# Feeding the first passes of a fused gated-MLP and spectral-filter kernel: two columns ahead of the rest, all their weights at once, the other columns transposed by DMA, and a deviation by square root and reciprocal

## The chip, the cores and the metric

One Trainium2 chip, one core. The time is the device time of one execution in microseconds (us), as the median of a kernel's runs. The profile gives one execution in full: its span is about 1.7 us shorter than the time. With each kernel under test the kernel before is run on the same chip, so each comparison has its own runs of before.

## The reference

```python
def reference(A_x, A_w_r, A_w_i, B_x, B_w_gate, B_w_up, B_w_down):   # helpers written inline
    x = A_x                                     # 1 x 2048 x 512, bf16
    xn = (x - mean(x)) / sqrt(var(x) + 1e-5)    # over the last axis
    X = rfft2(xn) * (w_r + 1j * w_i)            # spectral filter
    A = irfft2(X)
    g = xn @ B_w_gate                           # 512 x 1792
    u = xn @ B_w_up
    B = (gelu_tanh(g) * u) @ B_w_down           # 1792 x 512
    return x + A + B
```

The 2048 rows lie on 128 partitions in 16 "columns" of 128 rows. Both branches read the normalized rows: the gated MLP needs them transposed (`xnT`), the spectral branch reads them as they are, in four "folds" of four columns, and multiplies the folds (`xf`) with a table `RF_t` into `bp`.

## The kernel before

All five engines are planned by a small scheduler in the kernel: each operation has an estimated duration and a priority, the planner simulates the engines and the fetches, and the operations are emitted in the order that comes out. A changed estimate anywhere can therefore change the order of an engine much later. The parts that the change touches:

```python
    load_x(0, 1)
    d_ident = load_ct("ident", "ident", "ACT")
    load_x(1, 1)
    load_w(0, 2, ("SP", "ACT"))          # two chunks of gate and up weights a fetch
    add("ACT", 1.3, lambda: nc.scalar.activation(out=eps[:, 1:2], in_=eps[:, 0:1], func=AF.Gelu_apprx_tanh),
        (o_eps,), -900)                  # loads gelu's table early
    load_x(2, 2)
    load_w(2, 4)
    load_w(4, 6)
    load_x(4, 4)
    load_w(6, 10)
    load_x(8, 4)
    load_w(10, 14)
    # ... (cut)
    NWARM, NGAP, GAP = 10, 1, 4          # dummy matmuls: 10 of 512 at the start, 4 of 128 at column 0
    # ... (cut)
    def layernorm(c0, n, due, after=(), halves=1):
        # ... (cut: bn_stats and bn_aggr of each column, VectorE)
        e = dve(0.07, lambda: V.tensor_scalar(out=ve[:, k], in0=mv[:, k, 1], scalar1=EPS, ...), ag, due - 5)
        r = add("POOL", 0.55, lambda: nc.gpsimd.tensor_tensor(
            out=rstd[:, k], in0=ve[:, k], in1=half[:, k], op=ALU.pow), (e, o_mem[1]), due - 5, lag=0.1)
        # ... (cut: (x - mean) * rstd into xn, VectorE)
    # ... (cut: pe_transpose: four transposes into ONE tile, copied out by ScalarE and VectorE in halves)
    for c in range(4):
        if c == 2:
            layernorm(2, 2, -22, XT[0])
        pe_transpose(c, -28 + 3 * c)
        if c < NGAP:
            dummies(GAP, -29.9 + 3 * c, XN[c], P)
    for c0, n, due in ((4, 2, 14), (6, 2, 16), (8, 4, 24), (12, 4, 32)):
        layernorm(c0, n, due)
        for c in range(c0, c0 + n):
            dma_transpose(c, due)
        if c0 == 6:
            d_rf = load(P * NC * P * 2, lambda: nc.sync.dma_start(out=RF_t[:], ...), XN[7])
            load_x(12, 4, deps=XN[7])
    # ... (cut)
    FIRST = [(0, 1, 0, 4), (1, 1, 0, 4), (0, 2, 4, 2), (2, 2, 0, 2), (2, 2, 2, 2), (2, 2, 4, 2)]
    for c, n, f, nf in FIRST + [(0, 4, f, 1) for f in range(6, NFC)]:
        glu(c, n, f, nf)                 # (first column, columns, first chunk of 128, chunks)
```

## Time and profile before

| kernel before | value |
|---|---|
| median of its first 3 runs | 179.28 us (179.19 to 179.54) |
| span of the profiled run | 177.6 us |
| TensorE busy | 98% |
| first 256-wide matmul, from which TensorE is dense | 11.53 us |
| last matmul starts | 174.70 us, 163.17 us later |
| from there to the end | 2.9 us |

The page, the start and the pace of TensorE are shown and read in the prediction below. A timeline line reads: start, duration, engine, source line, operation, output<-input; in brackets how long the engine was idle before and what ended it.

### The profile page before, as it was taken

What the parts mean: (1) busy time and instruction counts of PE and PEld (TensorE: products, weight loads), DVE (VectorE), ACT (ScalarE), POOL (GpSimd) and SP (SyncE); (2) the same over time, 40 slices, a digit from 0 to 9 for tenths busy, and PEclk for the clock granted to TensorE, in tenths of its full rate; (3) what the DMA queues carried; (4) which work ended last, traced back from release to release, by engine and by line L of the source; (5) the groups of instructions that cost most, each with busy time, mean ns of one, the idle gap of its engine ahead of it and who ended that gap; (6) DMA issues with size and microseconds to landing.
All of it is one profiled execution on the core that took longest, in us unless ns stands there. A gap on an engine that the chain in (4) does not pass through costs nothing.

```text
span 177.6 us, 3041 instructions
## 1 busy us (share of the span) xinstructions
PE 173.4 (98%) x1100; PEld 92.9 (52%) x1100; DVE 118.1 (66%) x266; ACT 87.4 (49%) x158; POOL 18.6 (10%) x33
## 2 busy tenths in 40 slices
PE   6999999999999999999999999999999999999993
PEld 2598545545554544554555455554445444544463
DVE  1869999999537995889999885336442541632522
ACT  3162437456789737999998855453111211211100
POOL 3212138743200000000000000000000000000000
PEclk9999999999999999999999999999999999999999
DMA  5999487999297001302211121100222221322212
GB/s 144 311 355 359 86 270 84 223 296 193 52 347 255 2 0 29 93 2 59 61 48 37 37 59 37 27 0 0 84 68 66 83 89 59 92 80 69 74 45 59
DMA packets 23182, 19.24 MB, mean 108 GB/s; under 512 B 8512, under 2 KB 21824, under 8 KB 23168
## 3 DMA queue, kind: packets, MB, share of 16 engines
q1 hardware_dynamic: 22176, 17.57, 35.0%
q0 software_dynamic: 320, 1.19, 3.1%
q10 hardware_dynamic: 672, 0.30, 0.6%
q8 instruction: 8, 0.13, 0.3%
q14 instruction: 6, 0.05, 0.1%
HBM read 13.28 MB, written 2.10 MB: 87 GB/s over the span
## 4 chain that ended last, share of the span: by engine, by line
PE 91%; ACT 3%; DVE 3%; issue 1%; POOL 0%; DVEq 0%; POOLq 0%
PE u_ps L502 25%; PE g_ps L502 25%; PE warm L380 3%; ACT E L652 2%; PE yp L818 2%; PE bp L581 2%; PE gp L767 2%; PE yp__2078 L872 2%; PE yp__1994 L872 2%; PE yp__1967 L872 2%; PE yp__1936 L872 2%; PE yp__1909 L872 2%; PE yp__1820 L872 2%; PE yp__1793 L872 2%; PE yp__1762 L872 2%; PE yp__1735 L872 2%
## 5 line engine op out<-in xcount | busy, mean ns | idle before, releaser
L502 PE MATMUL g_ps<-xnT,Wg_sb 128*128 128x512 bf16 (+2 forms) x264 | 58.1, 347 | 0.0
L502 PE MATMUL u_ps<-xnT,Wu_sb 128*128 128x512 bf16 (+2 forms) x264 | 57.9, 347 | 0.0
L527 DVE TENSOR_TENSOR hT<-u_ps,ge 128x512 bf16<-128x512 f32 x56 | 38.4, 685 | 17.5 <-PE u_ps L502 14.4
L519 ACT ACTIVATE ge<-g_ps 128x512 bf16<-128x512 f32 x56 | 33.5, 598 | 30.5 <-PE g_ps L502 26.5
L502 PEld LDWEIGHTS <-Wu_sb 128*128 128x128 bf16 x264 | 24.3, 98 | 22.3 <-DMA Wu_sb<-in_B_w_up_dram 0.2
L502 PEld LDWEIGHTS <-Wg_sb 128*128 128x128 bf16 x264 | 24.3, 98 | 20.7 <-issue 0.2
L872 PEld LDWEIGHTS <-hT 128*128 128x128 bf16 x252 | 23.0, 98 | 21.9
L824 ACT CAST yf<-yp 128x512 bf16<-128x512 f32 x16 | 9.3, 586 | 37.6 <-PE yp L818 37.6
L652 ACT CAST E<-ep 64x512 bf16<-64x512 f32 x32 | 18.5, 579 | 1.1 <-PE ep L646 0.7
L396 DVE BATCH_NORM_STATS2 st<-x_t 128x6 f32<-128x512 bf16 x16 | 10.5, 676 | 4.8 <-DMA x_t<-in_A_x_dram 4.8
L629 ACT CAST ds<-dp 128x512 bf16<-128x512 f32 x16 | 8.8, 589 | 1.1 <-PE dp L624 1.0
L773 ACT CAST Gs<-gp 128x512 bf16<-128x512 f32 x16 | 8.6, 593 | 1.0 <-PE gp L767 1.0
L406 POOL TENSOR_TENSOR rstd<-ve,half 128x2 f32<-128x2 f32 (+2 forms) x7 | 6.6, 949 | 21.9 <-DVE ve L404 21.9
L585 ACT CAST Bs<-bp 128x512 bf16<-128x512 f32 x16 | 8.3, 603 | 0.5 <-PE bp L581 0.5
L818 PEld LDWEIGHTS <-Gs 128*128 128x128 bf16 x64 | 4.8, 98 | 3.5
L380 PE MATMUL warm<-warm 128*128 128x512 bf16 (+1 forms) x14 | 5.1, 539 | 1.3 <-POOL half L373 1.3
L412 DVE TENSOR_SCALAR xn<-x_t,mv,rstd 128x512 bf16<-128x512 bf16 (+1 forms) x17 | 6.1, 399 | 0.3 <-POOL rstd L406 0.3
L818 PE MATMUL yp<-CT,Gs 128*128 128x128 bf16 x64 | 6.0, 219 | 0.0
L683 DVE TENSOR_TENSOR m<-X,TW 128x1024 bf16<-128x1024 bf16 x8 | 5.5, 692 | 0.2
L624 PEld LDWEIGHTS <-Bs 128*128 128x128 bf16 x64 | 4.4, 98 | 2.4
L689 DVE TENSOR_TENSOR m<-X,TW 128x1024 bf16<-128x1024 bf16 x8 | 5.5, 684 | 0.0
L646 PE MATMUL ep<-ds,CT 128*128 128x512 bf16 x16 | 5.4, 379 | 0.0
(103 smaller groups left out, 169.0 us busy)
## 6 DMA issues: line engine op xcount, KB each, us to landing
y<-in_A_x_dram SPq DMA_DIRECT2D x16, 128.0 KB, 2.1
F<-F SPq DMA_DIRECT2D x32, 64.0 KB, 2.0
out_dram<-y SPq DMA_DIRECT2D x15, 128.0 KB, 1.7
Wd_sb<-in_B_w_down_dram SPq DMA_DIRECT2D x2, 896.0 KB, 8.3
x_t<-in_A_x_dram SPq DMA_DIRECT2D x3, 512.0 KB, 6.8
Wg_sb<-in_B_w_gate_dram SPq DMA_DIRECT2D x2, 512.0 KB, 6.8
Wu_sb<-in_B_w_up_dram SPq DMA_DIRECT2D x2, 512.0 KB, 9.1
Wg_sb<-in_B_w_gate_dram SPq DMA_DIRECT2D x3, 256.0 KB, 5.1
```

The costliest lines, as they stand in the source:

```text
L380: nc.tensor.matmul(tiles["warm"][:, 0:w], lhsT=warm[:, 0:P], rhs=warm[:, 0:w], start=True, stop=True)
L396: V.bn_stats(out=st[:], in_=x_t[:, c])
L502: nc.tensor.matmul(tiles[f"{nm}.{key}"][:, f * w:f * w + w], lhsT=W[:, e, (f0 + f) * P:(f0 + f + 1) * P], rhs=rhs(e), start=(f + e == 0), ...
L519: nc.scalar.activation(out=e[:, 0:nf * w], in_=tiles[f"g_ps.{key}"][:, 0:nf * w], func=AF.Gelu_apprx_tanh)
L527: V.tensor_tensor(out=out, in0=tiles[f"u_ps.{key}"][:, 0:nf * w].rearrange("p (f w) -> p f w", w=w) if nf > 1 else tiles[f"u_ps.{key}"][:, ...
L585: nc.scalar.copy(out=o, in_=tiles[f"bp.{cg}.{q}"][:].rearrange("p c (r g a) -> p (c r) g a", r=2, a=4))
L629: nc.scalar.copy(out=ds[:].rearrange("p (s k t) -> p s k t", s=2, t=2), in_=tiles[f"dp.{G}"][:].rearrange("p s t k -> p s k t"))
L652: nc.scalar.copy(out=tiles[f"E.{g}"][64 * h:64 * h + 64, r], in_=tiles[f"ep.{g}.{h}"][64 * r:64 * r + 64])
L773: nc.scalar.copy(out=o, in_=tiles[f"gp.{g}.{h}"][:].rearrange("p q (n a) -> p (q n) a", a=4))
L818: nc.tensor.matmul(yp[:, q], lhsT=tiles["G"][:, q, c], rhs=IQ[q], start=(q == 0), stop=(q == 3), skip_group_check=True)
L824: nc.scalar.copy(out=tiles[f"yf.{c // 2}"][:, c % 2], in_=tiles[f"yp.{c}"][:])
L872: nc.tensor.matmul(y[:, s], lhsT=tiles[sb, f][:, cl * P:(cl + 1) * P], rhs=Wd_sb[:, f, s], start=(f == 0), stop=False)
```

## The change

The intent: get TensorE dense sooner. Columns 0 and 1 come first with all 14 weight chunks (two columns wide after the first four), then columns 2 and 3 with all of theirs, two columns wide (the later blocks of four columns stay four wide); weights come in fetches of four chunks, gate ahead of up; column 0's deviation no longer goes through GpSimd's power; each half of a column has its own transpose tile; columns 2 and 3 are transposed by DMA instead of TensorE; x of columns 4 to 15 and `RF_t` are fetched after those transposes. Not shown in the cuts: in a pass of several chunks the matmuls of the first half of the contraction come first, the gathers of the filter's tables are planned behind the transposes of columns 12 to 15, and the weights of the last product (`Wd_sb`) come in one fetch.

```diff
-    def op(self, eng, dur, fn, deps=(), prio=0.0, new=(), use=(), lag=0.0, nbytes=0):
+    def op(self, eng, dur, fn, deps=(), prio=0.0, new=(), use=(), lag=0.0, nbytes=0, land=0.0):
 ... (cut: a fetch may be given the time at which the planner is to take it as landed)
-    load_x(2, 2)
-    load_w(2, 4)
-    load_w(4, 6)
-    load_x(4, 4)
-    load_w(6, 10)
-    load_x(8, 4)
-    load_w(10, 14)
+    d_g = [load_first(e, eng) for e, eng in ((0, "ACT"), (2, "SP"))]
+    add("ACT", 1.5, lambda: nc.scalar.activation(out=eps[:, 1:2], in_=eps[:, 0:1], func=AF.Sqrt), (o_eps,), -900)
+    d_u = load(NE * P * P * 4, lambda: nc.sync.dma_start(out=Wu_sb[:, :, 0:4 * P], ...), land=7.0)
+    load_w(4, 8, (8.4, 10.9), lambda: load_x(2, 2, 9.6))
+    load_w(8, 12, (12.2, 13.6))
+    load_w(12, 14, (14.3, 15.0))
 ... (cut)
-    NWARM, NGAP, GAP = 10, 1, 4
+    NWARM, NGAP, GAP = 8, 1, 2
 ... (cut)
+    def layernorm_sqrt(c, due, after=()):
+        s = dve(0.6, lambda: stats(c), [XD[c]] + list(after), due - 3.0)
+        a = dve(0.15, lambda: V.bn_aggr(out=mv[:, c], in_=tiles["st", c][:]), (s,), due - 3.2)
+        r = SD[c] = act(0.2, lambda: nc.scalar.activation(
+            out=rstd[:, c:c + 1], in_=mv[:, c, 1:2], func=AF.Sqrt, bias=eps[:, 0:1], scale=1.0), (a, o_eps), due - 60)
+        r = dve(0.07, lambda: V.reciprocal(out=rstd[:, c:c + 1], in_=rstd[:, c:c + 1]), (r,), due - 3.0)
 ... (cut: normalize in two halves; a transpose tile for each half)
+    layernorm_sqrt(0, -28)
+    layernorm_sqrt(1, -25, XN[0])
+    pe_transpose(0, -28)
+    dummies(GAP, -29.9, XN[0], P)
+    act(1.5, lambda: nc.scalar.activation(out=eps[:, 1:2], in_=eps[:, 0:1], func=AF.Gelu_apprx_tanh), [SD[1]] + XT[0], -70)
+    pe_transpose(1, -25, 1)
+    for c0, n, due in ((2, 2, -40), (4, 2, 14), (6, 2, 16), (8, 4, 24), (12, 4, 32)):
+        layernorm(c0, n, due, XN[max(c0 - 4, 1)])
         for c in range(c0, c0 + n):
             dma_transpose(c, due)
-        if c0 == 6:
+        if c0 == 2:
+            load_x(4, 4, 0.0, deps=XN[3], prio=-80.0)
+            load_x(8, 4, 0.0, deps=XN[3], prio=-80.0)
             d_rf = load(P * NC * P * 2, lambda: nc.sync.dma_start(
-                out=RF_t[:], ...), XN[7])
-            load_x(12, 4, deps=XN[7])
+                out=RF_t[:], ...), XN[3], prio=-80.0)
+            load_x(12, 4, 0.0, deps=XN[3], prio=-80.0)
 ... (cut)
-    FIRST = [(0, 1, 0, 4), (1, 1, 0, 4), (0, 2, 4, 2), (2, 2, 0, 2), (2, 2, 2, 2), (2, 2, 4, 2)]
-    for c, n, f, nf in FIRST + [(0, 4, f, 1) for f in range(6, NFC)]:
-        glu(c, n, f, nf)
+    for c in range(2):
+        glu(c, 1, 0, 4)
+    for f in range(4, NFC, 2):
+        glu(0, 2, f, 2)
+    for f in range(0, NFC, 2):
+        glu(2, 2, f, 2)
```

## The prediction

> **What bounds the kernel now.** I read the page first (busy shares, the strip of 40 slices, the chain by engine), then the groups by shape, then the timeline of TensorE alone over the first 60 us and the last ten, then the timeline of all engines over the first 9 us, last the DMA windows of 1 us.
>
> The page says that one engine is the kernel:
>
> ```profile
> PE 173.4 (98%) x1100; PEld 92.9 (52%) x1100; DVE 118.1 (66%) x266; ACT 87.4 (49%) x158; POOL 18.6 (10%) x33
> PE   6999999999999999999999999999999999999993
> PE 91%; ACT 3%; DVE 3%; issue 1%; POOL 0%; DVEq 0%; POOLq 0%
> ```
>
> TensorE has work from the first slice to the last, so only its own work, its start and the tail can matter. Its timeline shows where it becomes dense:
>
> ```profile
> 5.78 0.65 PE L428 MATMUL tp<-CT,xn 128*128 128x128 bf16 x4
> 6.23 0.63 PE L380 MATMUL warm<-warm 128*128 128x128 bf16 x4
> 6.89 0.82 PE L502 MATMUL g_ps<-xnT,Wg_sb 128*128 128x128 bf16 x8
> ...
> 10.19 0.61 PE L502 MATMUL g_ps<-xnT,Wg_sb 128*128 128x128 bf16 x8
> 10.64 0.61 PE L502 MATMUL u_ps<-xnT,Wu_sb 128*128 128x128 bf16 x8
> 11.09 0.61 PE L428 MATMUL tp<-CT,xn 128*128 128x128 bf16 x8
> 11.53 1.04 PE L502 MATMUL g_ps<-xnT,Wg_sb 128*128 128x256 bf16 x8
> 12.41 1.04 PE L502 MATMUL u_ps<-xnT,Wu_sb 128*128 128x256 bf16 x8
> ...
> 18.52 1.03 PE L502 MATMUL g_ps<-xnT,Wg_sb 128*128 128x512 bf16 x4
> 19.38 1.03 PE L502 MATMUL u_ps<-xnT,Wu_sb 128*128 128x512 bf16 x4
> ```
>
> The starts give the pace of one matmul (the durations overlap): 512 wide (19.38 - 18.52)/4 = 0.216 us, 256 wide (12.41 - 11.53)/8 = 0.109, 128 wide (10.64 - 10.19)/8 = 0.056. After 11.53 the program holds 641 matmuls of 512, 79 of 256 and 286 of 128: 138.3 + 8.6 + 15.9 = 162.8 us. The last one starts at 174.70, which is 163.2 us after 11.53. So there is no gap over 0.4 us in all behind 11.53; the tail from 174.70 to the end at 177.6 is 2.9 us (last add, last store). What can be won lies ahead of 11.53. There the first column's way to TensorE counts:
>
> ```profile
> 3.51 0.69 DVE L396 BATCH_NORM_STATS2 st<-x_t 128x6 f32<-128x512 bf16 x1 [3.51 <-DMA x_t<-in_A_x_dram]
> 4.23 0.18 DVE L403 BATCH_NORM_AGGREGATE mv<-st 128x2 f32<-128x6 f32 x1
> 4.45 0.15 DVE L404 TENSOR_SCALAR ve<-mv 128x1 f32<-128x1 f32 x1
> 4.52 0.69 DVE L396 BATCH_NORM_STATS2 st<-x_t 128x6 f32<-128x512 bf16 x1
> 4.76 0.58 POOL L406 TENSOR_TENSOR rstd<-ve,half 128x1 f32<-128x1 f32 x1 [2.70 <-DVE ve L404]
> 5.24 0.18 DVE L403 BATCH_NORM_AGGREGATE mv<-st 128x2 f32<-128x6 f32 x1
> 5.38 0.60 DVE L412 TENSOR_SCALAR xn<-x_t,mv,rstd 128x256 bf16<-128x256 bf16 x2
> ...
> 6.47 0.37 ACT L431 COPY xnT<-tp 128x256 bf16<-128x256 bf16 x1 [3.29 <-PE tp L428]
> 6.88 0.29 DVE L431 COPY xnT<-tp 128x256 bf16<-128x256 bf16 x1 [0.83 <-ACT xnT L431]
> ```
>
> From the aggregate (ends 4.41) to the normalization (5.38) are 0.97 us, for an add and a power on GpSimd. The two copies out of one transpose tile run one after the other: the first starts only when all four transposes are done (6.43), the second waits for the first. Column 1's statistics (4.52) hide inside the wait for GpSimd.
>
> **What the Trainium skill says.** "TensorE: Matmul & The Clock Gate", Part 1, says that the array runs at half clock until an activity window of about 3.4 us was busy, and that the window runs free. The trace agrees: the first warm-up matmuls start 0.43 us apart, twice 0.216, and the 128-wide ones go from 0.11 to 0.056 apart near 7.3 us, in the first eight of g_ps. "ScalarE: Activation LUTs", What ACT_TABLE_LOAD costs, gives 1283 ns for a load plus a drain of about 1380 ns, and about 280 ns for a small ACTIVATE whose bias is a pointer. The trace has one load, 1.28 us from 1.69, and its ACTIVATE at 2.98, so no drain is seen behind an empty engine; that ACTIVATE, with an immediate bias, takes 0.20 us. "DMA: Bandwidth & Descriptors", Anatomy of one DMA, puts about 2.0 us fixed on each transfer beside the bytes, on the GpSimd path; here, from SyncE, 512 KB alone land in 3.7 us (RF_t), of which 1.5 us are bytes at 0.36 MB/us: near 2.2 us.
>
> **The change part by part.**
>
> 1. Work of TensorE. After the narrow passes, columns 0 to 3 had four passes two columns wide and then eight chunks four wide; now all the rest is two wide. 64 matmuls of 512 (13.81 us) become 128 of 256 (13.96): +0.15 us. Eight transposes go to DMA: -8 x 0.056 = -0.45 us. Warm-up shrinks from 10+4 to 8+2, off the path.
>
> 2. Deviation of column 0. Aggregate ends 4.41; the square root on ScalarE starts near 4.48 and takes about 0.28 (the skill's figure for a pointer bias; 0.20 in the trace for an immediate); hop 0.06 as between ScalarE and VectorE elsewhere; reciprocal 0.15, as the 128x1 TENSOR_SCALAR; dependent start 0.07 later: normalization at 5.05 in place of 5.38, 0.33 us sooner.
>
> 3. Each half has its own transpose tile. Transposes start near 5.45, the first half ends near 5.85 at half clock, ScalarE copies to 6.25, g_ps starts near 6.3 in place of 6.89. Sixteen g_ps follow (all four chunks, half of the contraction first). At half clock until 7.3 and full clock after it they end near 7.7.
>
> 4. Column 1. The order of VectorE in the changed kernel puts its statistics behind the normalization of column 0, so they are hidden no longer: normalization of column 0 leaves the engine at 5.57, statistics to 6.29, copy of the half of column 0 to 6.58, aggregate to 6.76, square root and reciprocal 0.64, normalization from 7.4; its first half is ready at 7.74, the transposes run from 7.8 to 8.1. The order of TensorE has u_ps of column 0 behind them. So TensorE waits about 0.1 us here, and then runs 48 matmuls of 128 (u, g, u), 2.7 us: the narrow part ends at 10.8.
>
> 5. Before, the narrow part with all its transposes ended at 11.53, of which 0.45 was the transposes of columns 2 and 3. From the end of the narrow part on the new kernel has 577 x 0.2158 + 207 x 0.109 + 286 x 0.056 = 163.0 us against 162.8. End: 10.8 + 163.2 + 0.15 + 2.9 = 177.05 in place of 177.6: -0.6 us, if nothing stalls.
>
> 6. Weights. One fetch is 512 KB of four chunks now, with rows twice as long. By the windows 0.52 MB had moved by 4.0 us and 0.36 MB/us were reached later; landing lags the bytes by 1.1 to 1.5 us (up chunks 2 and 3, 1.61 MB down the queue, ended a wait at 8.84, their bytes had moved by 7.55). Worked out so, the gate chunks 0 to 3 land near 6.0 (wanted 6.3), up near 7.5 (wanted 8.1), gate 4 to 7 near 9.1 (10.8), columns 2 and 3 of x near 9.8, up 4 to 7 near 11.4 (12.5, since the order runs both gate passes first), the last ones near 15.7 (18.6). None should stop TensorE.
>
> 7. Columns 2 and 3. Statistics from 9.8, power on GpSimd (0.70 in the trace), normalization done near 13.4; two DMA transposes at 1.2 us of issue and 3.4 us to landing (2.4 to 5.3) are in by 17.7 to 19.6. They are wanted when the two-wide passes of columns 0 and 1 end: 10.8 + 80 x 0.109 = 19.5. x of columns 4 to 15 and RF_t are queued behind: RF_t lands near 22.1, the first bp wants it at 16.2 us of TensorE work, 23.0. Column 7's transpose lands near 31.6, wanted at 32.6. All fit, by about 1 us each.
>
> 8. The filter. Its gathers are queued behind the last power of GpSimd, near 41 us in place of 27.4; its tables took 18 us from the first gather (27.4 to 45.5), so they are ready near 59, and VectorE reads them first after three passes of the third block, near 67. From there it has 21 multiplies at 0.60 and eight filter groups of about 3.6 (pace of the timeline), near 42 us of work in 44: tight, but the last gp is moved back too, to 121.
>
> **The rivals.**
> (a) A later stall eats the gain: the transposes of columns 2 and 3, RF_t or column 7 come late. For it: each margin is 1 us or less and DMA transposes here took up to 5.3 us. Against: order and loads look fitted to just these landings. It would make 178.9 to 180.5.
> (b) The clock gate opens one window later, because eight warm-ups end near 4.8 and TensorE then idles 0.6 us, where before it was fed to 5.61. Then g, tp and u of the start run at 0.11 apiece until 10.7 and the narrow part ends near 12.3: 1.5 us worse, near 180.2. For it: gaps that were not there; against: the engine is still busy most of the window from 3.9 to 7.3.
> (c) Column 1 is quicker than I think and the waits were worth more: the narrow part ends near 10.0 and the time is 177.8. For it: the old start has 1.2 us of holes and half-clock work between 5.78 and 11.09; against: column 1's serial chain in step 4.
> (d) The second table load delays gelu. It falls behind column 1's square root, 7.2 to 8.5, or 9.9 with a drain; the first bank it must free is wanted at 10.8. Worth nothing.
>
> **Range and chances.** Time is span plus about 1.7 (179.28 against 177.6). The sum says 178.7. I add 0.1 for rival (a) and take 178.8; (c) sets the low end at 177.7, (b) and (a) the high one at 180.3. Two per cent is 3.6 us, more than all holes of the start together; a loss of that size would need (a) and (b) at once. Faster 0.03, same 0.93, slower 0.04.
>
> **What would show each step.** Step 2: normalization of column 0 starts near 5.05. Step 3: g_ps near 6.3. Step 4: TensorE waits for column 1, and the first 256-wide g_ps starts near 10.8 (11.53 before). Step 5: the last matmul starts about 163.4 later. Rivals: a wait of TensorE on xnT, bp or Wu after that; 128-wide matmuls still 0.11 apart after 7.5. A first 256-wide matmul later than 11.3, or a hole over 0.5 us behind it, would make the prediction wrong.

## More of the kernel before

In VectorE's timeline, this is the first time it touches x of columns 4 to 7:

```profile
12.17 0.69 DVE L396 BATCH_NORM_STATS2 st<-x_t 128x6 f32<-128x512 bf16 x1 [1.26 <-DMA x_t<-in_A_x_dram]
```

And these are lines of the DMA queue of SyncE in the same kernel ("SPq"; the duration is the time to issue, not to land):

```profile
5.31 1.51 SPq L315 DMA_DIRECT2D x_t<-in_A_x_dram  x1
...
17.74 4.35 SPq L437 DMA_TRANSPOSE xnT<-xn  x3
22.14 0.57 SPq L453 DMA_DIRECT2D RF_t<-spec_rf  x1
```

The reader is to see that x of columns 4 to 7 is issued at 5.31, long ahead of the first DMA transpose at 17.74. VectorE waits 1.26 us for it at 12.17, early, when nobody waits for VectorE.

## The result, and the profile after

The changed kernel took 181.31 us (median of 6 runs, 180.99 to 182.04), the kernel before 179.45 (6 runs, 179.19 to 180.03). The ratio of the fast runs is 1.0109, 95% interval 1.008 to 1.0137. A ratio here is the mean time of one kernel's fast runs over that of the other's of the same rounds, so it is not quite the ratio of the medians quoted. The changed kernel is 1.1% slower: within 2%, but 1.0 us beyond the top of the predicted range.

The page of the changed kernel, answering to the three lines of the prediction:

```profile
PE 172.8 (96%) x1152; PEld 97.8 (54%) x1152; DVE 120.2 (67%) x269; ACT 87.8 (49%) x159; POOL 14.9 (8%) x31
PE   7899999989899999999999999999999999999993
PE 71%; DVE 14%; DMA 7%; issue 3%; SPq 2%; POOL 1%; ACT 1%; DVEq 0%; POOLq 0%
```

TensorE is still above 95%, so the busy share says almost nothing. The chain of waits says it: TensorE's share of it fell from 91% to 71%, and VectorE (14%) and DMA (7%) now stand in it. The strip (40 slices of 4.49 us) has an 8 in its ninth and eleventh slice, at 36 to 40 and 45 to 49 us, where the kernel before has only nines.

The start, in the timeline of all engines (three lines of VectorE, one of ScalarE, two of TensorE, one of its weight loads):

```profile
3.96 0.18 DVE L417 BATCH_NORM_AGGREGATE mv<-st 128x2 f32<-128x6 f32 x1
4.18 0.30 ACT L418 ACTIVATE rstd<-mv,eps 128x1 f32<-128x1 f32 x1 [0.99 <-DVE mv L417]
4.51 0.16 DVE L420 RECIPROCAL rstd<-rstd 128x1 f32<-128x1 f32 x1 [0.36 <-ACT rstd L418]
4.71 0.60 DVE L424 TENSOR_SCALAR xn<-x_t,mv,rstd 128x256 bf16<-128x256 bf16 x2
...
5.86 1.05 PE L526 MATMUL g_ps<-xnT,Wg_sb 128*128 128x128 bf16 x16
...
7.16 0.54 PE L452 MATMUL tp<-CT,xn 128*128 128x128 bf16 x4 [0.24 <-DVE xn L424]
...
7.82 0.90 PEld L526 LDWEIGHTS <-Wu_sb 128*128 128x128 bf16 x16 [0.30 <-DMA Wu_sb<-in_B_w_up_dram]
```

The start did what it was meant to do. From the aggregate's end (4.14) to the normalization (4.71) are 0.57 us in place of 0.97. The first real matmul is at 5.86 (6.89 before), and the first 256-wide one at 10.52 (11.53 before). That is 1.0 us gained, of which 0.3 comes from x of column 0 landing sooner in this run. The last line is a wait of 0.30 us for the first up weights; in the two repeats below it is not there, and their first 256-wide matmul starts at 10.23 and 10.36.

It was lost behind it. The last matmul starts at 176.69, which is 166.17 us after 10.52. The prediction counted 163.0 us of work for that stretch. TensorE's timeline shows where the rest went:

```profile
21.00 1.04 PE L526 MATMUL g_ps<-xnT,Wg_sb 128*128 128x256 bf16 x8
22.62 1.03 PE L526 MATMUL u_ps<-xnT,Wu_sb 128*128 128x256 bf16 x8 [0.59 <-DVE hT L551]
23.83 1.05 PE L608 MATMUL bp<-RF_t,xf 128*128 128x128 bf16 x16 [0.17 <-DMA RF_t<-spec_rf]
...
37.46 0.40 PE L608 MATMUL bp<-RF_t,xf 128*128 128x128 bf16 x4 [0.40 <-DVE xf L590]
...
49.27 0.84 PE L608 MATMUL bp<-RF_t,xf 128*128 128x128 bf16 x12 [0.43 <-DVE xf L594]
```

The bracket counts idle time from the modelled end of the last matmul; the hole in the pace of starts is a little longer. Eight matmuls of 256 from 21.00 at 0.109 end their turn at 21.87, so the hole before 22.62 is 0.75 us. Worked out in this way the holes are 0.75 at 22.62, 0.34 at 23.83, 0.56 at 37.46, 0.39 at 38.07, 0.22 at 46.73, 0.60 at 49.27 and 0.26 at 86.83: 3.1 us, the 166.17 less 163.0. Only the last one stood in the kernel before (0.28 us at 76.21).

What made them is in VectorE's timeline:

```profile
21.29 0.70 DVE L401 BATCH_NORM_STATS2 st<-x_t 128x6 f32<-128x512 bf16 x1 [2.76 <-DMA x_t<-in_A_x_dram]
```

in SyncE's queue:

```profile
8.54 1.58 SPq L325 DMA_DIRECT2D Wu_sb<-in_B_w_up_dram  x1
13.18 3.55 SPq L462 DMA_TRANSPOSE xnT<-xn  x2
16.78 1.06 SPq L317 DMA_DIRECT2D x_t<-in_A_x_dram  x2
```

and in the table of windows (columns: stretch and its length, busy time and instructions of TensorE, its weight loads, VectorE, ScalarE and GpSimd, then granted clock, busy share of the DMA engines and GB/s):

```profile
16.00:17.00 1.00, 1.00 (x12) 0.90 (x10) 0.97 (x2) 0.17 (x1) 0.00 (x0) 1.00 0.61 62
...
20.00:21.00 1.00, 1.00 (x12) 0.89 (x11) 0.00 (x0) 0.60 (x1) 0.00 (x0) 1.00 0.96 356
```

SyncE's queue stands from 10.12, when the last weight fetch is issued, to 13.18: the next in its order are the two DMA transposes, and they wait for VectorE to normalize columns 2 and 3. Then they hold the queue to 16.73, the first for 2.25 us and the second for 1.30; the median of this kernel's 14 transposes is 1.22, and why the first took a microsecond more is not shown (the last weights were still moving, 330 and 282 GB/s from 13 to 15). From 16 to 17, when the weights are through, the DMA engines move 62 GB/s. x of columns 4 to 7 is issued behind them at 16.78 and lands near 21.3; `RF_t` is issued at 17.88 and lands near 23.8. VectorE, whose next instruction in its order is the statistics of column 4, stands still for 2.76 us. The multiply `hT` that follows it, whose `u_ps` was complete near 19.4, runs only at 21.90 and ends at 22.58, and at 22.62 TensorE gets the bank (the buffer into which `u_ps` is written) back. After that VectorE is busy almost without a pause until 52 (it caught up near 45 in the kernel before), and each `bp` finds its fold late.

### The profile page after: what moved, and what is told of

It is laid out like the page before. It is cut to its first block, busy times and chain, and to the rows that moved or that the text cites. A ratio compares the mean times of both kernels' runs of the same rounds, so it can differ in the third digit from the quotient of the medians.

```text
span 179.6 us, 3150 instructions
## 1 busy us (share of the span) xinstructions
PE 172.8 (96%) x1152; PEld 97.8 (54%) x1152; DVE 120.2 (67%) x269; ACT 87.8 (49%) x159; POOL 14.9 (8%) x31
## 4 chain that ended last, share of the span: by engine, by line
PE 71%; DVE 14%; DMA 7%; issue 3%; SPq 2%; POOL 1%; ACT 1%; DVEq 0%; POOLq 0%
PE u_ps L526 17%; PE g_ps L526 16%; DVE hT L551 4%; DMA x_t<-in_A_x_dram 4%; DMA RF_t<-spec_rf 3%; DVE st L401 2%; PE yp L845 2%; PE gp L794 2%; PE yp__2105 L899 2%; PE yp__2078 L899 2%; PE yp__2047 L899 2%; PE yp__1962 L899 2%; PE yp__1931 L899 2%; PE yp__1904 L899 2%; PE yp__1872 L899 2%
## 5 line engine op out<-in xcount | busy, mean ns | idle before, releaser
L526 PE MATMUL g_ps<-xnT,Wg_sb 128*128 128x512 bf16 (+2 forms) x296 | 57.5, 327 | 0.1
L526 PEld LDWEIGHTS <-Wu_sb 128*128 128x128 bf16 x296 | 27.3, 98 | 20.1 <-issue 1.1
L526 PEld LDWEIGHTS <-Wg_sb 128*128 128x128 bf16 x296 | 27.3, 98 | 18.9 <-issue 0.2
L401 DVE BATCH_NORM_STATS2 st<-x_t 128x6 f32<-128x512 bf16 x16 | 10.8, 674 | 6.2 <-DMA x_t<-in_A_x_dram 6.2
L867 DVE TENSOR_TENSOR lv<-yf 128x512 bf16<-128x512 bf16 x8 | 3.4, 423 | 7.8 <-ACT yf L851 7.1
L430 POOL TENSOR_TENSOR rstd<-ve,half 128x2 f32<-128x2 f32 (+1 forms) x5 | 4.9, 978 | 37.5 <-DVE ve L409 37.5
L436 DVE TENSOR_SCALAR xn<-x_t,mv,rstd 128x512 bf16<-128x512 bf16 x14 | 5.3, 426 | 0.9 <-POOL rstd L430 0.9
L608 PE MATMUL bp<-RF_t,xf 128*128 128x128 bf16 x64 | 4.6, 219 | 1.2 <-DVE xf L594 0.6
L845 PE MATMUL yp<-CT,Gs 128*128 128x128 bf16 x64 | 5.5, 219 | 0.0
```

The source lines that it names most:

```text
L401: V.bn_stats(out=st[:], in_=x_t[:, c])
L526: nc.tensor.matmul(tiles[f"{nm}.{key}"][:, f * w:f * w + w], lhsT=W[:, e, (f0 + f) * P:(f0 + f + 1) * P], rhs=rhs(e), start=(f + e == 0), ...
L845: nc.tensor.matmul(yp[:, q], lhsT=tiles["G"][:, q, c], rhs=IQ[q], start=(q == 0), stop=(q == 3), skip_group_check=True)
```

## The experiments

**The changed kernel again.** No edit.

> The changed kernel again, as the reference for the other runs on the same chip. Near 181.3 us, about 1.0% over the kernel before; holes of TensorE at about 22.6 (0.75 us), 23.8 (0.35) and 37 to 49 us (together about 1.8).

Measured: 181.11 us (median of 6, 180.71 to 182.53), before 179.33; ratio 1.0104, interval 1.0076 to 1.0133. The same holes, 0.65 us of wait at `u_ps` near 22.5 and the others, stand in its trace. The loss is real and its places are steady.

**x of columns 4 to 7 not waited for (wrong result).** The statistics and the normalization of columns 4 to 7 read x of columns 0 to 3, which has long been there. The order on all five engines is the same as in the changed kernel, the fetches too.

```diff
-        V.bn_stats(out=st[:], in_=x_t[:, c])
+        V.bn_stats(out=st[:], in_=x_t[:, c - 4 if 4 <= c < 8 else c])
-                    out=xn[:, c, d], in0=x_t[:, c, d], ...
+                    out=xn[:, c, d], in0=x_t[:, c - 4 if 4 <= c < 8 else c, d], ...
```

> Columns 4 to 7 are normalized from the data of columns 0 to 3, which landed long before (wrong result on purpose); the order of all engines and all transfers stay the same, only VectorE's wait for that x goes. Theory 1 (the late x of columns 4 to 7 blocks VectorE's queue for 2.8 us, and VectorE then lags until about 52 us): the hole at 22.6 moves into the wait for RF_t, so bp still starts near 23.8, but the holes at 37 to 49 (1.8 us) vanish: near 179.5 us. Rival (the new order gives VectorE too much to do ahead of the folds, whenever x lands): the holes at 37 to 49 stay and the time stays near 181.2 us.

Measured: 180.32 us (179.83 to 181.51), ratio 1.0069 (1.0039 to 1.0099), 0.8 us under the changed kernel by the medians. The result is wrong (relative error 0.0202). The holes near 22.6, 37 and 46 are gone. Two are left in TensorE's timeline:

```profile
23.46 1.05 PE L608 MATMUL bp<-RF_t,xf 128*128 128x128 bf16 x16 [0.75 <-DMA RF_t<-spec_rf]
...
47.81 0.84 PE L608 MATMUL bp<-RF_t,xf 128*128 128x128 bf16 x12 [0.43 <-DVE xf L594]
```

Without VectorE's wait TensorE arrives sooner at the next late fetch, `RF_t`, and part of the gain turns into that wait: its hole there is 0.92 us in place of 0.34. The hole at the third fold stays: it does not come from the landing of x.

**The same, with `RF_t` in the queue slot of columns 4 to 7.** Wrong again; engine orders unchanged, only two fetches change places.

```diff
-            load_x(4, 4, 0.0, deps=XN[3], prio=-80.0)
+            (fetch RF_t here)
...
-            d_rf = load(... out=RF_t[:] ...)
+            (fetch x_t[:, 4:8] here)
```

> As the run with columns 4 to 7 from resident data, and RF_t is fetched in the place of those columns' x, two transfers earlier, the order of all engines unchanged. Theory 1: no hole over 0.3 us behind the narrow part; 181.3 - 3.1 us of holes + 0.3 = near 178.5 us, 0.5% below the kernel before, as the prediction's own sum had it without stalls. Rival: the holes at 37 to 49 stay, near 180.2 us.

Measured: 179.51 us (179.39 to 180.91), ratio 1.0033 (1.0004 to 1.0061); 1.6 us under the changed kernel. The only hole over 0.3 us left is that of the third fold, 0.59 at 47.33. So the two late landings are worth 1.6 us together, and what remains is near the kernel before, not below it.

**The planner told the true landing times.** Right result; only the estimates change, so the engine orders do.

```diff
-            load_x(4, 4, 0.0, deps=XN[3], prio=-80.0)
-            load_x(8, 4, 0.0, deps=XN[3], prio=-80.0)
+            load_x(4, 4, 20.9, deps=XN[3], prio=-80.0)
+            load_x(8, 4, 22.2, deps=XN[3], prio=-80.0)
 ... (RF_t 23.4, columns 12 to 15 24.6)
```

> Only the landing times that the order is planned from are changed, to what the trace shows (x of columns 4 to 7 at 21, 8 to 11 at 22, RF_t at 23.5, 12 to 15 at 24.5 us); loads and data as in the changed kernel, right result. Statistics of column 4 come two multiplies later on VectorE, the first bp behind two more passes on TensorE. Theory 1 in the form that the wait only hurts because work that is ready stands behind it: VectorE waits less, the holes at 22.6 and 23.8 (1.1 us) vanish and some of the later ones stay: 179.3 to 180.3 us. Rival (the data simply come too late for the columns 4 to 15, whatever the order): a hole of like size appears where column 7 or the later folds are wanted, near 181 us.

Measured: 180.72 us (180.46 to 182.3), ratio 1.0072 (1.0059 to 1.0085). The holes at 22 to 24 went, but later ones grew (0.97 at 39.70, 0.92 at 50.31, both waits for VectorE's `xf`): a better order moves the wait, it does not remove it. The profiled run was this kernel's slow one (182.3), and its TensorE timeline shows the prediction's rival (b):

```profile
6.43 1.87 PE L526 MATMUL g_ps<-xnT,Wg_sb 128*128 128x128 bf16 x16
8.09 0.64 PE L452 MATMUL tp<-CT,xn 128*128 128x128 bf16 x4
...
10.23 1.07 PE L526 MATMUL g_ps<-xnT,Wg_sb 128*128 128x128 bf16 x16
```

Sixteen 128-wide matmuls take 1.7 us up to 10.2 (0.107 apart) and 0.9 us after it. The first 256-wide one starts at 12.03; in the kernel with `RF_t` in another slot, whose first transposes came at the same time (5.57 and 5.58), it starts at 10.67. So the late gate costs 1.36 us here. "Slow run" means in this text the upper of two groups of a kernel's runs; these runs are less than 1.5% apart, and all count as of state fast.

**Warm-up of the kernel before put into the changed one.** Two wide and two narrow dummy matmuls more; the planner gives them no time, so the order of everything else stays as it is.

```diff
-    dummies(NWARM, -100)
+    dummies(NWARM, -100); [pe(0.0, lambda: warm_mm(D), [o_mem[0]], -99.9, use=(wb,)) for i in range(2)]
-    dummies(GAP, -29.9, XN[0], P)
+    dummies(GAP, -29.9, XN[0], P); [pe(0.0, lambda: warm_mm(P), [o_mem[0]] + XN[0], -29.85, use=(wb,)) for i in range(2)]
```

> The changed kernel with the warm-up of the kernel before (10 wide and 4 narrow matmuls in place of 8 and 2), nothing else moved. Theory 2 (in two of six runs of the changed kernel the clock of TensorE opens one activity window later, because TensorE stands idle between the shorter warm-up and the first transposes; the trace of the run with the landing times shows it, with 128-wide matmuls 0.107 us apart until 10.2): no run over 181.9 us, all within about 0.8 us of each other, the fast ones not faster than 180.7. Rival (the slow runs come from the transfers or from a phase that the warm-up does not touch): about a third of the runs still 1.3 to 1.8 us above the others.

Measured: 182.25 us (181.42 to 182.95), before 179.96; ratio 1.0117 (1.009 to 1.0144). No gain and no narrower spread. The longer warm-up pushes the first transposes from 5.11 to 5.59, and a new hole of 0.90 stands at 54.22. This did not settle what the warm-up is worth.

**Columns 2 and 3 transposed by TensorE,** and x of columns 4 to 11 right behind the weights.

```diff
+    load_x(4, 4, 16.6)
+    load_x(8, 4, 18.0)
-            dma_transpose(c, due)
+            pe_transpose(c, due) if c0 == 2 else dma_transpose(c, due)
-            load_x(4, 4, 0.0, deps=XN[3], prio=-80.0)
-            load_x(8, 4, 0.0, deps=XN[3], prio=-80.0)
```

> Columns 2 and 3 transposed by TensorE again, and x of columns 4 to 11 fetched directly behind the weights; all else as in the changed kernel, right result. Theory 1: x of columns 4 to 7 lands near 17.5 us and RF_t before 23, so the holes at 22 to 24 vanish and the later ones shrink below 0.6 us in all; 0.45 us more work of TensorE: fast runs near 179.2 us (181.0 - 1.1 - 1.2 + 0.45), with the slow third of theory 2 still there, near 180.8. Rival (the order, not the landing, lets VectorE lag): 180.3 us or more in the fast runs.

Measured: 180.71 us (180.35 to 182.51), before 179.96; ratio 1.0044 (1.002 to 1.0069). No hole is left from 22 to 46 us, as the landing theory wants. The profiled run (182.51) opened its gate late again (first 256-wide matmul at 11.99), and behind 46 it has new holes at `bp` (1.23 at 51.64, and 0.75 more before 53.06), which wait for ScalarE's copies `Bs`. The same with the long warm-up and a plan made anew:

```diff
-    NWARM, NGAP, GAP = 8, 1, 2
+    NWARM, NGAP, GAP = 10, 1, 4
```

> The run with columns 2 and 3 on TensorE, and the warm-up of the kernel before. Theories 1 and 2 together: 179.0 to 179.4 us in all runs, equal to the kernel before within 0.2%; no slow third. If the front of the changed kernel is worth what the prediction said, 0.6 us less, near 178.8.

Measured: 182.65 us (4 runs, 182.28 to 183.04), ratio 1.0141. A miss of mine: the new plan put column 1's square root ahead of the copy that the first `g_ps` needs, so that one started at 7.17 after a wait of 0.89, and `bp` waits 2.04 us at 51.68. It says nothing on the warm-up.

**The power on GpSimd kept, all else changed.**

```diff
-        r = SD[c] = act(0.2, ... func=AF.Sqrt, bias=eps[:, 0:1] ...)
-        r = dve(0.07, lambda: V.reciprocal(...), (r,), due - 3.0)
+        e = dve(0.07, lambda: V.tensor_scalar(... scalar1=EPS ...), (a,), due - 5)
+        r = SD[c] = add("POOL", 0.55, lambda: nc.gpsimd.tensor_tensor(... op=ALU.pow), (e, o_mem[1]), due - 5, lag=0.1)
 ... (gelu's table loaded at the start, no second load)
```

> Square root and reciprocal undone: columns 0 and 1 take the power on GpSimd as in the kernel before, one table load; all else as in the changed kernel. If the start counts (both columns' deviations lie one after the other on the way to the narrow part), 0.4 us per column: near 181.8 us. If the later waits for x and RF_t, which land at a time set by the queue, swallow what the start wins: no change, near 181.1 us. The normalization of column 0 starts 0.9 to 1.0 us behind its aggregate, in place of 0.57.

Measured: 182.88 us (181.35 to 183.46), before 179.96; ratio 1.0141 (1.0102 to 1.018). In its profile the normalization starts at 5.57, 0.96 us after the aggregate's end at 4.61; with square root and reciprocal it is 0.57. That prices this part at 0.39 us of the start. The time can't be used for it: the profiled run opened its gate late (first 256-wide at 12.36), and the runs lie in two groups.

**The kernel before with square root, reciprocal and separate transpose tiles alone.** Loads, passes and TensorE's transposes of columns 2 and 3 as before.

```diff
-    first = layernorm(0, 1, -28, (), 2)
-    layernorm(1, 1, -25, first)
+    layernorm_sqrt(0, -28)
+    layernorm_sqrt(1, -25, XN[0])
 ... (one transpose tile a half; gelu's table loaded behind column 1's square root)
```

> The kernel before with only the second half of the change: deviation of columns 0 and 1 by square root and reciprocal, a transpose tile per half, gelu's table loaded afterwards; loads, passes and transposes of columns 2 and 3 as before, warm-up 10 and 4. If the prediction's steps 2 to 4 hold by themselves, TensorE's first 256-wide matmul starts 0.3 to 0.8 us sooner than before (11.53) and, with no new hole behind it, the time is 178.6 to 179.1 where before has 179.3. Rival: the start gain is paid back by a wait at 20 to 50 us because VectorE's order moves, so the time is that of before within 0.2.

Measured: 180.48 us (180.09 to 181.31), before 179.97; ratio 1.0032 (1.001 to 1.0055). A miss, and an instructive one. The first `g_ps` came at 6.46 in place of 6.89, and then TensorE ran into the weights:

```profile
8.41 0.62 PE L517 MATMUL g_ps<-xnT,Wg_sb 128*128 128x128 bf16 x8 [0.76 <-DMA Wg_sb<-in_B_w_gate_dram]
```

With the loads of before, the quicker deviation only makes TensorE wait longer for the next weight chunks. A hole of 1.10 at 14.86, where ScalarE's copy of columns 2 and 3 comes late in the new plan, did the rest (the profiled run, 181.31 us, was the slowest of the six). So this half of the change needs the other, the weight fetches; that the other needs this one is not shown.

**The kernel before with the short warm-up.** VectorE, ScalarE, GpSimd and the queue keep their order throughout, TensorE for its first 60 us.

```diff
-    NWARM, NGAP, GAP = 10, 1, 4
+    NWARM, NGAP, GAP = 8, 1, 2
```

> The kernel before with the changed kernel's short warm-up (8 wide and 2 narrow dummy matmuls in place of 10 and 4) and nothing else in the first 60 us moved. Theory of the clock gate (the shorter warm-up makes the gate open a whole window late in some runs): a part of the runs, some 2 to 4 of 6, comes 1 to 1.8 us above the others, near 181, and a profile of such a run shows 128-wide matmuls still 0.11 us apart after 8 us; the median may rise by up to 1. Rival (the split of the changed kernel's times has nothing to do with the warm-up): all runs within 0.9 us of each other as before, and the median within 0.3 of before.

Measured: 179.76, 179.90, 181.34, 182.11, 182.24 and 182.28 us in six runs, where before had eleven between 179.49 and 180.42. Two groups, as the theory of the clock gate has it; but the gap of 1.5 to 2.5 us is more than it said. The profiled run was a fast one. Two more (before 179.36):

> The kernel before with the short warm-up, one look. If this run is a slow one (near 182): by the theory of the clock gate, 128-wide matmuls lie 0.107 apart until past 10 us and the first 256-wide one starts near 12.8 to 13; by the rival the pace is 0.056 from 7.3 on and a wait of TensorE for a fetch or an engine, of over 1 us, stands in its timeline.

> As e11b, a second look, because about two runs in three are slow.

Measured: 180.24 and 179.90 us. The first one has the late gate in TensorE's timeline:

```profile
6.59 1.12 PE L502 MATMUL g_ps<-xnT,Wg_sb 128*128 128x128 bf16 x8 [0.25 <-ACT xnT L431]
7.51 1.06 PE L502 MATMUL u_ps<-xnT,Wu_sb 128*128 128x128 bf16 x8
...
12.39 1.04 PE L502 MATMUL g_ps<-xnT,Wg_sb 128*128 128x256 bf16 x8
```

Eight matmuls from 7.51 take 0.86 us to the next start (8.37), 0.107 apart, where the kernel before ran at 0.056 from about 7.3. The first 256-wide matmul is at 12.39 in place of 11.38 in the profiled fast run: 1.0 us. The second had its gate in time and two short waits for weights. So the gate can open late with the short warm-up, and that made this run 0.9 us slower than before. The four upper runs lie 1.4 to 2.3 us over their kernel before, more than that, and have no profile; what else is in them stays open.

**x of columns 4 to 7 ahead of the two DMA transposes.** Right result; the planner knows of it.

```diff
     load_w(12, 14, (14.3, 15.0))
+    load_x(4, 4, 16.6)
...
-            load_x(4, 4, 0.0, deps=XN[3], prio=-80.0)
```

> The changed kernel with x of columns 4 to 7 put into the queue ahead of the two DMA transposes of columns 2 and 3. Theory 1 (those loads stand behind the transposes and hold VectorE): x of columns 4 to 7 lands before 19, the holes at u_ps near 22.6 and bp near 37 to 47 shrink by 1 us or more, time 0.8 to 1.6 us under the changed kernel (179.6 to 180.4). Against that the transposes land 1 to 1.5 us later, near 19.5, wanted at about 19.3, a hole of 0.2 to 1 us at the first pass of columns 2 and 3 and RF_t near 24. Rival (VectorE's order itself, not the landing, makes the holes): the same holes as in the changed kernel and the same time within 0.4 us.

Measured: 179.32 us (178.81 to 179.51), before 179.97; ratio 0.9962 (0.9942 to 0.9982). The first kernel under the kernel before.

> The changed kernel unchanged, on the chip of the next run. As before: 1.0 to 1.4% above the kernel before, most runs within 0.7 us and about one in four 1 to 1.5 us above those.

> The same kernel as e3 (x of columns 4 to 7 ahead of the two DMA transposes). Theory 1: 1.8 to 2.6 us under the changed kernel on the same chip. Rival (the second chip, not the order, made e3 fast): within 1 us of the changed kernel. If the clock gate is a matter of the short warm-up alone, about one run in four is 1 to 1.5 us slower, as in the changed kernel.

Measured: changed kernel 180.93 us (180.53 to 182.6), ratio to before 1.011 (1.0074 to 1.0146); x first 179.28 us (178.76 to 180.4), ratio 0.9997 (0.9972 to 1.0023); before 179.36. So the place of one fetch in the queue, with the plan that goes with it, is worth 1.65 us by the medians. In the profile of x first, 164.11 us lie between the first 256-wide matmul (10.52) and the last, in place of 166. `RF_t` is the largest wait left (in the profile of the first call it was the transpose of column 2, a hole of 0.46 at 19.80, as that expectation feared):

```profile
23.53 1.05 PE L608 MATMUL bp<-RF_t,xf 128*128 128x128 bf16 x16 [0.31 <-DMA RF_t<-spec_rf]
```

**Landing or order?** The planner had also changed the order of VectorE and TensorE. Two kernels take the two apart: the early fetch with the engine orders of the changed kernel, and the new orders with the late fetch. In both only the queue differs from the kernel that it is taken from.

```diff
 (early fetch, old order)
-            load_x(4, 4, 0.0, deps=XN[3], prio=-80.0)
+            (planned as before, issues nothing)
+            (behind the last weight fetch: nc.sync.dma_start(out=x_t[:, 4:8], in_=x_v[:, 4:8]))
 (late fetch, new order)
-    load_x(4, 4, 16.6)
+    (planned as before, issues nothing)
+    (behind the transpose of column 3: nc.sync.dma_start(out=x_t[:, 4:8], in_=x_v[:, 4:8]))
```

> The changed kernel, all engines in its own order, x of columns 4 to 7 issued ahead of the two DMA transposes. Theory 1 (landing): VectorE's wait of 2.8 us at 21.3 shrinks under 1, the hole at u_ps near 22.6 is gone, those at 37 to 47 go for the most part as in e1, the hole of 0.5 to 0.6 at the third fold stays as in e1 and e2; time 1.0 to 1.6 us under the changed kernel, ratio to before 1.001 to 1.005. Rival (order): holes as in the changed kernel, ratio 1.008 to 1.012.

> The engine orders of e3, but x of columns 4 to 7 fetched behind the transposes as in the changed kernel. Theory 1 (landing): VectorE waits for x until 21 as before and TensorE has holes near 22 to 24 and 36 to 50 of 1.5 to 3 us in all, ratio to before 1.006 to 1.012. Rival (order): ratio 0.996 to 1.000 as e3.

Measured: early fetch with the old order 180.42 us (180.01 to 181.82), ratio 1.003 (0.9974 to 1.0087); late fetch with the new order 181.85 us (181.58 to 182.49), ratio 1.0095 (1.0043 to 1.0146). Three of the eleven runs of before lay at 181.2 to 181.6, which widens both intervals; the spans of the profiled runs are clearer:

| | x of columns 4 to 7 behind the transposes | ahead of them |
|---|---|---|
| order of the changed kernel | span 179.6, 179.4, 179.2; ratio 1.0109, 1.0104, 1.011 | span 178.5; ratio 1.003 |
| order planned for the early fetch | span 180.1; ratio 1.0095 | span 177.7, 177.5; ratio 0.9962, 0.9997 |

SyncE's queue and VectorE with the early fetch and the old order:

```profile
10.05 1.35 SPq L326 DMA_DIRECT2D x_t<-in_A_x_dram  x1
...
18.50 0.68 DVE L401 BATCH_NORM_STATS2 st<-x_t 128x6 f32<-128x512 bf16 x1
```

The fetch is issued 6.7 us sooner, and no wait stands at the statistics: the 2.76 us are gone. TensorE with the late fetch and the new order:

```profile
22.48 1.03 PE L526 MATMUL u_ps<-xnT,Wu_sb 128*128 128x256 bf16 x8 [2.20 <-DVE hT L551]
```

The new order alone makes the hole larger (2.2 us of wait in place of 0.6), because it puts the statistics even earlier. With the early fetch the order is worth about 1 us of span: the old order still has 0.59 at 47.38 (VectorE's `xf`) and 0.76 at 52.08 (ScalarE's `Bs`), the new one has neither. The rival "order instead of landing" falls; the landing is the condition, and the order adds to it. The evidence is of two strengths: with the new order the late fetch costs 2.4 us of span and the intervals of the ratios lie apart (1.0043 to 1.0146 against 0.9942 to 0.9982 and 0.9972 to 1.0023); with the old order the interval of the early fetch still holds the ratio of the changed kernel, so there it rests on the traces, and on the 0.8 us of the run in which x was not waited for.

## Why the prediction was wrong

The step that failed is step 7, in what it left out: VectorE's wait for the fetches queued behind the transposes. The steps in order:

Step 1, the work of TensorE, held: the holes worked out one by one (3.1 us) add up to what the 166.17 us have over the 163.0 counted.

Step 2, the deviation of column 0, held: 0.57 us from aggregate to normalization where the step had 0.64 and the kernel before 0.97. The square root took 0.30 us (0.28 estimated), the reciprocal 0.16.

Steps 3 and 4 held. `g_ps` came at 5.86 where 6.3 was said, with x 0.3 us sooner in that run; in the run of x first, where x came as in the kernel before (statistics at 3.53), it was 6.26. TensorE waited for column 1 (0.24 us), and the narrow part ended at 10.52 in both (10.8 said).

Step 5 is the sum "if nothing stalls". In place of 163.35 us behind the narrow part the trace has 166.17. (The sum took the measured 163.2 of the kernel before, with its 0.4 us of gaps, and added 0.15; that is why it is above the 163.0 counted.)

Step 6 held behind 10.52: no matmul waited for a weight fetch there. Ahead of it "None should stop TensorE" was not quite so: the first up weights, said near 7.5, held their weight load for 0.30 us until 7.82 in this profile, though not in the two repeats.

Step 7 failed. It had the two transposes issued in 1.2 us each, and they took 2.25 and 1.30; it had `RF_t` land near 22.1, and it landed near 23.8, wanted at 23.0 by its own count. Its landings of the transposes held: the first pass of columns 2 and 3 started at 19.25 without a wait. These errors of size were the small part. "All fit, by about 1 us each" was said of TensorE's needs alone. The step did not ask who else reads these fetches: VectorE takes x of columns 4 to 7 in its own order, ahead of a multiply that frees TensorE's bank, and so waited 2.76 us. The early fetch with all orders unchanged removed that wait (span 178.5 in place of 179.2 to 179.6), so this part is shown. In the same way the later holes near 37 are its debt, for they go when x is not waited for. The hole of about 0.6 at the third fold does not go with the landing: it stays in every run that keeps VectorE's order and is gone in the profiles of x first, where the order is another. No step of the prediction followed VectorE's order from 23 us to the filter.

Step 8, the filter, held: its gathers start at 44.6 (41 said), and nothing waited for its tables.

Of the rivals, (a) was right in kind and given 0.1 us where it cost 1.65 with the order that goes with it. Its evidence was listed in the prediction (a transpose that took 5.3 us, margins of 1 us) and then discounted with "order and loads look fitted to just these landings". They were fitted in the planner's model, which took the landing from the bytes alone. Rival (b) is likely to be in it too: 5 of 18 runs of the changed kernel lie at 182.0 to 182.6, the others have a mean of 180.97, so the slow ones add (182.26 - 180.97) x 5/18 = 0.36 us to the mean. No slow run of the changed kernel itself was profiled; in the three variants of it whose slow run was (true landings, TensorE's transposes, power on GpSimd), it was the late gate. That the short warm-up alone makes it frequent is not shown: with the same warm-up the x first kernel had one slow run in 12, and the kernel before with its long one had three runs 1.5 us or more above its median in the last call. Rival (c), a narrow part that ends near 10.0, came in part: 10.52, and 10.23 and 10.36 in the repeats, where 10.8 was said. Rival (d), the second table load, cost nothing, as said.

What is left of the 181.3 against 178.8: with x first the kernel ran at 179.3, which is 0.5 above the prediction. Its trace has 164.11 us behind the narrow part (0.76 more than 163.35) and a narrow part that is 0.28 shorter, which is 0.48. The rest, 1.65 us in the same call, is step 7; and the first call's median was 0.4 above that of the later one.

## What to carry to other kernels

When fetches are moved behind others in one queue, list for each one every engine that reads it, in that engine's own order, and ask what stands behind the read; a fetch that the bottleneck wants late may be wanted early by an engine that frees the bottleneck's buffers. A margin of 1 us against a landing time that the trace itself shows to vary by 3 us is no margin, and a gain of 0.6 us should be weighed against all such margins together. When a start becomes quicker, move the fetch that the next engine wants as well: here one line, a 512 KB fetch ahead of two DMA transposes, with the order planned from it, turned 1.1% slower into level with or 0.4% faster than the kernel before.

## What the Trainium skill lacked or had wrong

- "Advanced Engine Details and Errata", X-Bar Transpose (TRN2), says that transpose DMAs are as fast as regular ones, with 350 to 400 GB/s to be expected. Four transposes of 128 KB from SBUF to SBUF, back to back, held the issuing queue for 5.12 us from 34.54 on in the changed kernel, 102 GB/s; the two that matter here held it for 3.55, and the DMA engines moved 62 GB/s in a window with them against 356 with ordinary fetches. That the queue is held, so that fetches behind it are issued late, is what that page lacks, and it is a part of what cost most. "DMA: Bandwidth & Descriptors" lists cycles of the issuing sequencer for transposes of "previous generations", in a part on trn3, but no time for one of this size on trn2.
- "ScalarE: Activation LUTs", What ACT_TABLE_LOAD costs, has a drain of about 1380 ns beside the load. The second load here, straight behind an ACTIVATE (6.22 to 6.51), ran from 6.54 to 7.82, and the next ACTIVATE started at 7.83: no drain. Its figure for a small ACTIVATE with a pointer bias, about 280 ns, agrees with 0.30 us here.
- "TensorE: Matmul & The Clock Gate", Part 1, calls the ramp's cost under 1% and variable between runs. The traces agree: a late opening moved the first 256-wide matmul by 1.0 and 1.36 us in two profiles, 0.6 and 0.8% of this kernel. What it lacks is how often: 5 of 18 runs of the changed kernel lay 1.3 us above the rest, though only variants of it show the late gate in a profile.
- No page says that the granted clock of a profile does not show this gate: it reads 1.0 in the run whose 128-wide matmuls lay 0.107 us apart until 10.2. The spacing of starts shows it.
